# A new hand-written order of steps for a fused attention and ReGLU kernel, and a separate buffer for its last output columns

## The chip, the cores and the metric

The kernel runs on one core of a Trainium2 chip. The metric is the device time of one execution in microseconds (us). A core has five engines that run side by side, each working through its own queue of instructions in order: TensorE (PE in the profile; its weight loads are PEld), VectorE (DVE), ScalarE (ACT), GpSimd (POOL) and SyncE (SP, which here only issues transfers). Transfers issued by SP and ACT show in the profile as hardware queues (q1, q10), those issued by POOL as the software queue (q0).

## The reference

```
def phi(x):
    proj = np.einsum('bhsd,df->bhsf', x, w_phi)            # d = 64, f = 128
    proj = proj - np.max(np.abs(proj), axis=-1, keepdims=True)
    return np.concatenate([np.exp(proj), np.exp(-proj)], axis=-1)
q_p, k_p = (phi(q), phi(k))                                # q, k, v: [8, 8, 576, 64]
kv = np.einsum('bhsf,bhsd->bhfd', k_p, v)
z = np.sum(k_p, axis=2)
num = np.einsum('bhsf,bhfd->bhsd', q_p, kv)
den = np.einsum('bhsf,bhf->bhs', q_p, z)[..., None] + 1e-06
x = (num / den).transpose(0, 2, 1, 3).reshape(4608, 512)
out = (np.maximum(x @ w_gate, 0) * (x @ w_val)) @ w_out    # 512 -> 1536 -> 512
```

Eight batches of linear attention with an exponential feature map feed a gated feed-forward layer over 4608 tokens. Inputs and output are float32; the products run in bfloat16.

## The kernel before, in words

The work is cut into 1427 small steps. The code registers them under keys, such as `("fv", 1, 0)`, and a string `ORDER` of step numbers (a planner searched it by annealing under a cost model of its own) says in which order they are written into the program. Each step puts its instructions at the end of the queues of the engines that it uses, so `ORDER` fixes the order inside each engine, and the engines wait for each other through semaphores. A mark `'` behind a number takes the step's other engine, where it has two. A word `z4` puts four dummy matmuls on zeros there.

Steps by key, with their lines in the profile:

- `ld`: a load. `v` and `vm` (value rows) are issued by SP; `k`, `q`, `km`, `qm` and the weights (`wv0` to `wv2`, `wg0` to `wg2`, `wo`) by POOL, since they are cast to bfloat16 on the way (L214, L220, L236, L243, L252). Batch 0's k and v are loaded ahead of the order, by SP, k in float32 into the buffer that v of batch 1 takes afterwards. `v2` takes the buffer of `v0`.
- `turn`: a transpose of q or k by DMA, issued by SP (batches 2 to 7, L292, and the tails, L298). Batches 0 and 1 are turned on PE (`kT`, `qT`, L271) and copied out of PSUM (`kTc`, `qTc`, L284, on DVE or ACT).
- `kr`, `qr` (L312), `qc` (L543): the feature products on PE; `km`, `qm` (L319): row maxima on DVE; `ke`, `qe` (L368, L561): the exponentials on ACT; `kk`, `qk` (L379, L577): the exponentials `ek`, `cq` of the maxima on ACT.
- `vs`, `vsm` (L328, L410, L395): value rows times `ek`, the "scalings", on POOL or DVE. Both operands lie in SBUF.
- `kv` (L482, L505): PE sums keys times values; `kvc` (L418) copies the sums out on ACT or DVE.
- `n` (L591): PE products of queries with those sums; `nt`, `nu` (L610, L622) combine them on DVE; `xu` (L629, L631): a reciprocal on DVE and the division on POOL or DVE; `xd` (L639): a DMA transpose of the result into `xT`, issued by SP (batches 0 and 1 use PE, `xT` and `xc`, L271 and L651).
- `fv`, `fg` (L721, with the copy L736 on ACT or DVE, and L743 on DVE): the value and the gate half of the first feed-forward product, for group g of 512 tokens and one of 12 slices of 128 columns. Group 0 runs its first eight pairs on 256 tokens each; its pairs 0 to 7 read `wv0` and `wg0`, 8 to 11 `wv1` and `wg1`, 12 to 15 `wv2` and `wg2`.
- `fo` (L769, copy L779, store L750 or L754): the second product, in three thirds of four matmuls for each 128 tokens. Groups 0 to 7 are the batches' first 512 tokens; group 8 takes the last 64 of every batch, and its last 128 tokens are done in two parts, columns 0 to 351 and 352 to 511.

The attention of batch b + 1 is laid between the feed-forward products of group b, so PE's queue alternates between both. `out_sb`, which holds output rows until they are stored, has two buffers in turn.

Of the kernel before, what the change touches and what calls it, by code (L numbers as in the profile page):

```python
# [8 lines left out]
FP32 = mybir.dt.float32  # L9
# [13 lines left out]

ORDER = """7 z4 82 92 8 83' 93' 84 87 86 88 94 97 95 99 100 98 96 0 85 89 102 103 101' z1 104 108 105 90' z1
112 122 106 107 109 29 110 113' 114 111' 115 123' 124 118 126 132 127 117 119 91 128 133 125 120 z3
148 149 187 188 134 137 135 116 129 156 151 160 155 158 153 121 10 130 142 143' 131 190 192 136 139
144' 194 150 152 157 161 138 140 154 196 159 198 189 191 200 141 145 147' 162 1 146 54 193 175 176
163 266 267' 164 177 2 195 165 166 169 170 167 171 168 181 182 199 3 226 172 178 214 201 179 183 9  # L30
# [5 lines left out]
284 288 1118' 1119 286 1120 1121 274 292 323 325 285 287 289 265 264 279 280 361 363 281 327 276  # L36
291 360 365 278 277' 293 30 295 329 333 1122 297 303 296 304 298 305 331 39 312 1123 1124 300 301
335 348 351 299 302 352 353 51 313 349 364 366 314 1125 306 1126 315 316 317 342 354 355 350 356 12
357 362 1127 1128 343 344 309 310 311 318 1129 367 368 373 358 359' 374 375 369 339 340 40 1130
# [9 lines left out]
522 515 491 521 493 520 494 1171 1172' 492 1173 1174' 1175 19 1176 516 519 570 574 572 495' 528 532  # L49
# [3 lines left out]
543 549 1189 1190 1191 636 638 550 599 598 603 551 602 1192' 1193 1194 601 582 583 561 562 637 579  # L53
580 600 1195 1196 640 605 604 639 641 606 607 584 1197 1198 1199 626 630 581 72 585 586 616 617 646
650 1200 620 36 1201 629 618 45 643 647 649 651 652 1202 1203 648 608 1204 1205 35 627 631 619 621
609 691 610 623 695 663 667 628 22 46 657 622' 661 659 1206 1207 632 611 665 653 612 693 613 614
1208 1209 1210' 662 666 615 656 660 692 1211 1212' 696 694 658 56 664 1213 1214 1215 624 625' 633
634 635 736 737 697 701 698 700 642 1216' 1217 740 73 644 645' 699 680 739 654 655 1218 702 675 668
681 682 721 703 722 723 738 1219 1220 672 676 1221 669 673 677 707 683 684 21 674 708 670 671 678
679 685 718 719 720 1222 1223 1224 1225 1226 25 741 742 686 687 688 709 743 1227 715 716 717 689'  # L60
690 1228 766 768 756 53 757 23 770 746 747 749 748 1229 1230 760 1231 1232 710 750 704 705 706 711
1233 759 1234 712 713 1235 751 752' 773 775 714 724' 725 761 763 726 802 804 1236 1237' 728 730
1238 1239 777 727 729 1240 1241 731 806 732' 758 767 772 776 771 762 801 769 1242 1243' 753 744
745' 805 754 774 803 764 765 755 733 734 735' 37 837 808 810 807 812 841 809 1244' 1245 1246 813 48
47 820 821 1247 778 811 1248 26 839 814 815 816 785 786 822 817 818 787 779 780 781 819 1249 796
1250 1251 1252 797 836 840 838 74 798 77 823 824 75 1253 790 791 1254' 1255 793 24 794 795 76 831
# [5 lines left out]
935 939 881 964 1287 906 81 966 967 968 28 50 965 937 1288' 1289 934 1290 1291 1292 936 974 977 976  # L72
870 938 940 941 975 994 1293 997 862 863 852 996 872 873 978 995 882 883' 1294' 1295 1296 979 981
907 908 999 910 942 943 1297 853 1000 944 998 913 914 909 915 969 1298 1299 945 1300 911 912 916
921 922 924 925 1301 948 1001 980' 1302 1303 1304 949 57 917 926 946 918 1002 1003 923 950 947 959
919 1305 960 956 920 927 928 961 957 958 1306 971 982 983 951' 952 953 984 986 988 954 955 1004
# [43 lines left out]
def kernel(  # L120
# [32 lines left out]
    E = D + 1  # L153
# [11 lines left out]
    sb_f = ctx.enter_context(tc.tile_pool(name="sb_f", bufs=3))  # L165
# [5 lines left out]
    sb_g = ctx.enter_context(tc.tile_pool(name="sb_g", bufs=4))  # L171
# [540 lines left out]
    def ffn(g):  # L712
# [45 lines left out]
        for t in range(4):  # L758
            cols = LAST if g == B and t == 3 else ((0, DM),)
            for part, (c0, c1) in enumerate(cols):  # L760
                for third in range(3):

                    @atoms.add("fo", g, t, part, third)
                    def _(alt, t=t, part=part, third=third, c0=c0, c1=c1):
# [14 lines left out]
                        copy_by(copy_of(alt, "ACT", "DVE"))(out_sb, po)  # L779
                        store(t, out_sb, c0, c1)  # L780

# [25 lines left out]

    atoms.run(ORDER, keep_busy)
# [28 lines left out]
```

## Time and profile before

| | us |
|---|---|
| median of 3 runs (385.54 to 386.85) | 385.89 |
| the profiled execution's own time | 386.66 |
| its span, first to last instruction | 384.9 |
| PE busy | 365.2 (95%) |
| DVE busy | 298.4 (78%) |
| ACT busy | 223.3 (58%) |
| POOL busy | 140.8 (37%) |

Busy time is the time in which an engine had an instruction in work; PE's includes 9 dummy matmuls, and the ends of matmuls are modelled.

### The profile page before, as it was taken

To read this page: it belongs to the slowest core of one execution; us is meant where nothing else is said; L and a number is where in the kernel's file an instruction comes from. 1 tells how busy PE (TensorE), PEld (TensorE's weight loads), DVE (VectorE), ACT (ScalarE), POOL (GpSimd) and SP (SyncE) were. 2 spreads that over 40 slices of the span, in tenths; PEclk is the share of its full clock that TensorE was granted. 3 is DMA by queue.
4 is the path that set the end of the run, shared out by engine and by line. 5 is a ranking of instruction groups with operands and counts; after the bars stand their busy time and mean duration, and the time that the engine had idled before them with its cause. 6 is when DMAs were issued, how large, how long until landed. Compare 5 with 4: busy or idle time off the path is not lost.

```text
span 384.9 us, 8951 instructions
## 1 busy us (share of the span) xinstructions
PE 365.2 (95%) x3457; PEld 196.2 (51%) x3505; DVE 298.4 (78%) x639; ACT 223.3 (58%) x524; POOL 140.8 (37%) x178
## 2 busy tenths in 40 slices
PE   6779999999998999899999999999999999999995
PEld 2567455545544645465555544455554544444443
DVE  7998897988888899888998897998958734834520
ACT  7898794769476847874875539774663403201111
POOL 5775742447462327742550227815501110000000
PEclk9899999999999999999999999999999999999999
DMA  8999993995199994974947825863310130021003
GB/s 256 186 240 207 206 153 78 211 175 103 52 187 164 186 153 72 165 136 114 147 119 160 178 29 151 164 98 42 96 56 3 28 111 27 2 66 57 2 17 93
DMA packets 87930, 45.11 MB, mean 117 GB/s; under 512 B 55824, under 2 KB 82000, under 8 KB 87888
## 3 DMA queue, kind: packets, MB, share of 16 engines
q1 hardware_dynamic: 60208, 30.42, 35.8%
q0 software_dynamic: 27200, 13.57, 28.1%
q8 instruction: 27, 0.44, 0.5%
q10 hardware_dynamic: 480, 0.56, 0.5%
q14 instruction: 15, 0.12, 0.1%
HBM read 37.78 MB, written 9.44 MB: 123 GB/s over the span
## 4 chain that ended last, share of the span: by engine, by line
PE 83%; DVE 6%; DMA 5%; ACT 3%; issue 2%; POOL 1%; SPq 0%; DVEq 0%
PE pa L721 47%; PE pa L769 21%; PE pa L591 5%; PE pa L482 4%; PE pa L312 3%; DMA wg_sb<-in_moe_w_gate_dram 3%; DMA xT<-xu 2%; PE pa L543 2%; ACT kp L368 2%; DVE vs L328 2%; DVE mk L319 1%; DVE t L610 1%; DVE u L622 1%; DMA out_dram<-out_sb 1%; DVE mq L319 1%
## 5 line engine op out<-in xcount | busy, mean ns | idle before, releaser
L721 PE MATMUL pa<-xT,wv_sb 128*128 128x512 bf16 (+1 forms) x384 | 98.3, 370 | 2.6 <-DMA xT<-xu 1.4
L721 PE MATMUL pa<-xT,wg_sb 128*128 128x512 bf16 (+1 forms) x385 | 97.7, 370 | 2.1 <-DVE h L743 0.8
L769 PE MATMUL pa<-wo_sb,h 128*128 128x512 bf16 (+2 forms) x429 | 97.4, 373 | 1.2 <-issue 0.5
L743 DVE SCALAR_TENSOR_TENSOR h<-pa,val_sb 128x512 bf16<-128x512 f32 (+1 forms) x112 | 74.2, 668 | 31.4 <-PE pa L721 26.1
L736 ACT CAST val_sb<-pa 128x512 bf16<-128x512 f32 (+1 forms) x75 | 43.0, 573 | 82.1 <-PE pa L721 81.1
L561 ACT ACTIVATE qp<-pa 128x512 bf16<-128x512 f32 x144 | 76.7, 626 | 9.9 <-PE pa L543 7.7
L368 ACT ACTIVATE kp<-pa 128x512 bf16<-128x512 f32 (+1 forms) x152 | 77.4, 593 | 8.1 <-PE pa L312 7.3
L631 POOL TENSOR_TENSOR xu<-u,r 128x512 bf16<-128x512 f32 x30 | 31.1, 1040 | 135.3 <-DVE r L629 72.2
L328 POOL TENSOR_TENSOR vs<-vn,ek 128x512 bf16<-128x512 f32 (+1 forms) x58 | 59.4, 1036 | 33.7 <-ACT ek L379 30.5
L721 PEld LDWEIGHTS <-wv_sb 128*128 128x128 bf16 x448 | 41.8, 98 | 46.5 <-DVE mk L319 1.9
L721 PEld LDWEIGHTS <-wg_sb 128*128 128x128 bf16 x448 | 41.6, 98 | 45.8 <-issue 2.1
L769 PEld LDWEIGHTS <-h 128*128 128x128 bf16 x444 | 41.2, 98 | 46.0 <-issue 1.1
L319 DVE TENSOR_REDUCE mk<-pa 128x4 f32<-128x512 f32 (+1 forms) x76 | 46.8, 650 | 3.9 <-PE pa L312 3.3
L319 DVE TENSOR_REDUCE mq<-pa 128x4 f32<-128x512 f32 x72 | 46.2, 677 | 2.7 <-PE pa L312 2.6
L610 DVE TENSOR_TENSOR t<-pa,cq 128x195 f32<-128x195 f32 (+3 forms) x120 | 38.0, 327 | 5.4 <-ACT cq L577 3.3
L622 DVE TENSOR_TENSOR u<-pa,t 128x195 f32<-128x195 f32 (+3 forms) x120 | 37.8, 332 | 2.9
L591 PEld LDWEIGHTS <-qp 128*128 128x128 bf16 x640 | 27.6, 98 | 14.3 <-issue 2.7
L779 ACT COPY out_sb<-pa 128x512 f32<-128x512 f32 x21 | 12.6, 599 | 38.1 <-PE pa L769 36.6
L591 PE MATMUL pa<-kv,qp 128*128 128x65 bf16 x640 | 30.4, 193 | 2.2 <-issue 1.4
L736 DVE CAST val_sb<-pa 128x512 bf16<-128x512 f32 (+1 forms) x37 | 25.0, 677 | 6.1 <-PE pa L721 5.5
L779 DVE COPY out_sb<-pa 128x512 f32<-128x512 f32 (+2 forms) x16 | 10.5, 653 | 24.1 <-PE pa L769 22.8
L482 PEld LDWEIGHTS <-kp 128*128 128x128 bf16 x480 | 16.1, 98 | 2.7 <-DVE kv L418 0.4
(68 smaller groups left out, 284.4 us busy)
## 6 DMA issues: line engine op xcount, KB each, us to landing
out_dram<-out_sb SPq DMA_DIRECT2D x32, 256.0 KB, 2.5
vn<-in_v_dram SPq DMA_DIRECT2D x6, 1024.0 KB, 6.5
qn<-in_q_dram POOLq DMA_DIRECT2D x8, 512.0 KB, 8.2
kn<-in_k_dram POOLq DMA_DIRECT2D x6, 512.0 KB, 7.8
wv_sb<-in_moe_w_val_dram POOLq DMA_DIRECT2D x3, 512.0 KB, 10.9
wg_sb<-in_moe_w_gate_dram POOLq DMA_DIRECT2D x3, 512.0 KB, 9.7
wo_sb<-in_moe_w_out_dram POOLq DMA_DIRECT2D x1, 1536.0 KB, 15.3
vn<-in_v_dram SPq DMA_DIRECT2D x1, 1152.0 KB, 7.9
```

Source lines behind the costliest of these rows:

```text
L319: nc.vector.tensor_reduce(m, some.rearrange("p (c f) -> p c f", f=F), axis=AX.X, op=ALU.max, apply_absolute_value=True,)
L328: eng.tensor_tensor(dst[:, :, s, 0:D], src, ek[:, :, s : s + 1].to_broadcast(list(src.shape)), op=ALU.mult,)
L368: nc.scalar.activation(st["kp"][:, s, 0 : n // 2, par, :], st["banks"][par][:, 0 : n // 2 * F].rearrange("p (a f) -> p a f", f=F), AF.Exp, ...
L482: nc.tensor.matmul(kv_ps[:, hh, s, :], lhsT=lhsT, rhs=rhs, start=(n == 0), stop=(n == 19))
L561: nc.scalar.activation(x["qp"][:, s, slot].rearrange("p a b -> p (a b)"), st["cols", i][par], AF.Exp, scale=sign,)
L591: nc.tensor.matmul(pn[:, E * (2 * i + s) : E * (2 * i + s + 1)], lhsT=x["qp"][:, s, slot, blk, :], rhs=kv_of(b, lo + i)[:, s, :],)
L610: nc.vector.tensor_tensor(x["t", j][rows, 0:n], ab[:, :, 1], c[:, :, None].to_broadcast([np_, n, E]), op=ALU.mult,)
L622: nc.vector.tensor_tensor(x["u"][rows, lo : lo + n], ab[:, :, 0], x["t", j][rows, 0:n], op=ALU.add)
L721: nc.tensor.matmul(ps, lhsT=w[:, dc, P * fi : P * fi + P], rhs=xTs[g][:, dc, lo:hi], start=(dc == 0), stop=(dc == NDC - 1),)
L736: copy_by(copy_of(alt, "ACT", "DVE"))(st["val", n], ps)
L743: nc.vector.scalar_tensor_tensor(st["h2"][:, fi, lo:hi], ps, 0.0, st["val", n], op0=ALU.max, op1=ALU.mult)
L769: nc.tensor.matmul(po, lhsT=st["h2"][:, fi, P * t : P * t + P], rhs=wo_sb[:, fi, c0:c1], start=(fi == 0), stop=(fi == NFC - 1),)
```

## The change

`ORDER` is replaced as a whole. The set of steps is the same, and so is the broad plan: counted along PE's queue, the first `fv` of every group stands within two matmul groups of where it stood. What differs is the order inside that plan, and the engine of some steps:

| steps | before | after |
|---|---|---|
| `kTc` on ACT / DVE | 8 / 3 | 5 / 6 |
| `kvc` on ACT / DVE | 19 / 13 | 12 / 20 |
| `fv` copies on ACT / DVE | 75 / 37 | 71 / 41 |
| `fo` copies on ACT / DVE | 21 / 16 | 22 / 15 |
| `xc` on ACT / DVE | 5 / 3 | 4 / 4 |
| `xu` division on POOL / DVE | 30 / 6 | 28 / 8 |
| `vs` on POOL / DVE | 58 / 12 | 59 / 11 |
| dummy matmuls | 4, 1, 1, 3 | 3, 1, 6 |

The planner that made the new order no longer lets a scaling on VectorE run while GpSimd works, and it serves transfers in order of their arrival.

The loads of the opening and of the second group in their order (P: POOL's queue, S: SP's queue; `xd 2 1` is a quarter of batch 2's result, the store is of group 1):

```
before  P: q0 k1 (vs 0 1 0) wv0 qm0 (vs 0 2 0) (vs 0 0 1) (vs 0 3 0, 0 3 1) q1 (vs 0 4 0 .. 0 5 1) wg0 wv1 wg1 (xu, xu) wv2 (xu, xu) wg2 wo k2
        S: turn-qm0 v1 turn-k2 ...        later: xd 2 1, v3, xd 2 0, turn-qm1, xd 2 3, store, xd 2 2
after   P: q0 k1 wv0 qm0 (vs 0 0 1) (vs 0 2 1, 0 2 0) (vs 0 3 0, 0 3 1) q1 (vs 0 4 0 .. 0 5 1) wg0 wv1 (xu, xu) wg1 km1 (xu, xu) wv2 wg2 wo k2
        S: turn-qm0 v1 vm1 v2 turn-km1 turn-k2 ...  later: v3, v4, xd 2 0, xd 2 2, store, xd 2 1, xd 2 3
```

The other edit gives the last 160 output columns a buffer of the pool of `u`, which is idle by then:

```
-                        out_sb = sb_g.tile([P, DM], FP32, name="out_sb", bufs=2)[:, 0 : c1 - c0]
+                        if part:
+                            out_sb = sb_f.tile([P, H, E], FP32, name="u").rearrange("p h e -> p (h e)")
+                        else:
+                            out_sb = sb_g.tile([P, DM], FP32, name="out_sb", bufs=2)
+                        out_sb = out_sb[:, 0 : c1 - c0]
                         copy_by(copy_of(alt, "ACT", "DVE"))(out_sb, po)
                         store(t, out_sb, c0, c1)
```

The start of the string, before and after:

```
-ORDER = """7 z4 82 92 8 83' 93' 84 87 86 88 94 97 95 99 100 98 96 0 85 89 102 103 101' z1 104 108 105 90' z1
+ORDER = """z3 82 83' 92 93' 94 97 7 8 98 95 99 84 87 86 96 0 102 103 88 85 z1 104 105 107 100' 122 112 89 90'
...
```

More of the change, by code (lines that the diff above doesn't have):

```diff
@@ L54 @@
[L54 to L65, printed above, removed]
@@ new lines @@
+163 164 177 195 199 31 166 167 169 170 168 165 178 256 226 227' 171 179 1 257' 2 172 181 182 180
+246 266 217 236 12 183 220 267 184 201 282 221 197 218 222 219 214 215 173 283' 205 237 216 321
+174' 185 186 322' 202 203 3 30 208 209 223 210 206 204 207 211 238 240 1092 1093 1094 239 4 247 242
+1095 1096 224 225' 1097 1098' 5 212 213 6 11 324 326 241 328 228 232 1099 1100 230 1101 1102' 229
+1103 1104 1105 1106 231 233 1107 1108 243 244 245 268 269 248 271 13 258 234 270 259 250 1109 262
+1110' 251 249 253 261 273 274' 263 272 1111 1112 252 1113 1114' 1115 264' 260 255 1116 1117 284 330
@@ new lines @@
+332 290 288 334 235 292 1118 294 1119 1120' 1121 286 254 323 327 285 289 287 276 361 363 278 277
+325 365 51 265 275 279 280 329 331 281' 291 39 295 360 40 293 296 1122 300 303 301 302 304 297 333
+298 305 299 306 1123 1124 335 354 355 356 312 313 351 1125 362 309 310 339 340 336 364 337 341 314
+307 308' 315 366 316 317 311 1126 1127 338 342 352 353 318 343 344 345 367 368 369 348 373 374 349
+1128 375 1129 319 320' 1130 1131 350 1132 357 378 398 401 379 382 14 381 408 410 400 41 16 42 358
+359 1133 1134 409 346 347 402 1135 399 411 413 414 370 371 380 372 1136' 412 1137 1138' 1139 58 60
@@ new lines @@
+59 403 388 425 427 429 1140 389 62 391 1141 1142 1143 393 383 404 61 33 52 1144 1145 1146' 392 419
[5 rows of a table added]
+1167 514 55 499 19 510 537 529 533 503 502 44 534 536 488 491 1168' 1169 1170 531 490 515 564 568
+492 518 520 538 521 489 493 505 519 1171' 522 523 504 506 507 494 1172 1173 1174 528 532 530 570
+574 516 517' 572 566 575 1175 1176 1177 569 573 571 66 525 69 67 71 563 567 1178' 1179 524 526 43
+527' 540 1180' 544 495 496 565 35 376 547 548 549 497' 558 559 560 1181 590 68 545 546 70 1182 1183
+591 1184 555 556 593 557 552 22 541 542 20 553 554 587 588 592 561 562 594 595 589 1185 1186 1187
@@ new lines @@
+1188 543 1189 550' 598 602 599 551 601 600 636 603 604 1190' 1191 639 1192 579 1193 638 1194' 1195
+637 640 1196 580 576 577 578 46 596 641 605 606 607 582 583 584 34 1197 597 643 1198 1199 626 581
+585 586 646 649 648 627 629 647 628 616 630 1200 1201' 1202 651 652 608 45 620 617 619 377 1203
+1204 1205 609 621 610 1206 663 618 667 691 56 657 695 622 661 650 1207' 665 1208 1209 653 611 612
+1210' 642 623 631 633 659 693 613 614 615 1211 1212 1213 1214' 662 664 656 692 694 36 666 1215 696
+1216' 1217 658 668 660 1218' 698 700 697 699 736 740 72 624 625' 737 654 655 702 739 23 644 632 634
@@ new lines @@
+635' 701 645' 1219 1220' 703 707 708 672 715 718 716 741 709 717 1221 53 721 719 722 720 1222 723
+738 680 681 675 724 676 1223 686 687 688 21 677 710 25 1224 682 1225 1226 711 673 674 725 712 669
+670 671 743 1227 1228 766 768 73 756 759 746 749 1229 47 1230' 678 679 760 770 1231 758 748 683 684
+685 704 705 706 1232 747 751 752 757 1233 1234 1235 689 726 801 803 690 805 802 727 761 729 728
+713' 714 1236 1237' 806 750 804 730 753' 1238 1239 731 733 1240' 767 769 771 773 754 732 755 1241
+1242 1243 775 777 734 808 37 810 772 776 774 807 811 763 1244' 48 1245 1246 742 812 813 735 762 764
@@ new lines @@
+765' 809 1247 744 74 745 78 836 837 75 839 76 1248' 841 1249 1250 828 77 79 81 820 829 830 1251 817
+814 815 816 1252 1253 840 825 1254 818 821 838 831 832 27 822 826 827 819 38 57 782 1255 1256 1257
+1258 778 833 790 779 780 783 784 834' 842 849 850 851 1259 1260 1261 1262 781 1263 846 28 847 793
[4 rows of a table added]
+1285 50 1286' 1287 1288 880' 964 967 965 935 939 930 932 934 937 966 892 893 968 862 1289 1290' 863
[3 rows of a table added]
+955 970 921 922 923 927' 928 1304 1305 951 952 1306 1004 1008 984 987 985 1006 1046 956 989 957 991
@@ new lines @@
+1048 1050 958 962 963 986 1307 1308 1002 1003 979 1309' 1310 1010 1014 1005 1009 980 981 1012 988
+1040 1044 1042 1007 1311 1312 1051 982 983' 972 973' 1011 1015 1045 1039 1047 990 1049 1041 1313
+1043 992 993' 1013 1016 1314 1315 1316 1317 1318' 1319 1020 1069 1070 1320' 1017 1018 1019 1071
+1063 1064 1065 1023 1321 1024 1025 1066 1067 1322 1021 1022 1026' 1027 1323 1324 1325 1068 1034
+1035 1036 1055 1326 1327 1328' 1074 1078 1076 1075 1329 1056 1052 1053 1330' 1057 1331 1332 1031
+1032 1058 1059 1060 1333 1334 1054 1061 1062 1335 1336' 1337 1338' 1339 1028 1072 1073 1029 1030
@@ L91 @@
+1033 1037 1038 1340 1341 1342' 1343 1344 1345 1346 1347 1348 1087 1349 1077 1079 1080 1350 1351
[4 rows of a table added]
+1418 1419 1420 1421 1422 1423 1424 1425 1426'"""
 class Atoms:
```

27 lines of the change are left out of this document (3 added, 24 removed), and 42 rows, old and new, of the table ORDER.

## The prediction

> **What bounds the kernel now.** I read the busy times first, then the busy time of each engine by stretches of 10 us, then every idle gap of PE after the opening.
>
> ```profile
> PE 365.2 (95%) x3457; PEld 196.2 (51%) x3505; DVE 298.4 (78%) x639; ACT 223.3 (58%) x524; POOL 140.8 (37%) x178
> ...
> 10.00:20.00 10.00, 7.82 (x149) 5.16 (x150) 10.00 (x18) 8.75 (x25) 7.86 (x11) 0.83 1.32 183
> 20.00:30.00 10.00, 8.04 (x193) 6.57 (x193) 9.20 (x32) 10.00 (x24) 6.01 (x9) 1.00 1.22 244
> ...
> 110.00:120.00 10.00, 8.44 (x67) 3.89 (x66) 8.38 (x15) 8.22 (x23) 5.24 (x7) 1.00 1.01 171
> ...
> 350.00:360.00 10.00, 9.95 (x48) 4.52 (x47) 6.39 (x10) 1.17 (x2) 0.00 (x0) 1.00 0.07 28
> ```
>
> The last four rows give, after the length, the busy time of PE, PEld, DVE, ACT and POOL, PE's granted clock, the DMA share and GB/s. From 10 to 30 us PE is busy 15.9 of 20 us while DVE and ACT reach 10.00 of 10: there the attention's vector work sets the pace. Later PE is full (9.95 in 350 to 360), and only a gap in PE's work, or less of it, moves the end. The new order has the same matmuls but one dummy more. So its whole possible gain lies in the opening, in the gaps, and behind the last matmul. The gaps above 0.3 us (in brackets, with what ended them):
>
> ```profile
> 30.68 0.61 PE L721 MATMUL pa<-xT,wg_sb 128*128 128x256 bf16 x4 [0.36 <-DMA wg_sb<-in_moe_w_gate_dram]
> 58.58 0.64 PE L591 MATMUL pa<-kv,qp 128*128 128x65 bf16 x15 [1.37 <-issue]
> 118.01 1.02 PE L721 MATMUL pa<-xT,wv_sb 128*128 128x512 bf16 x4 [1.41 <-DMA xT<-xu]
> 160.16 1.02 PE L721 MATMUL pa<-xT,wg_sb 128*128 128x512 bf16 x4 [0.37 <-DVE mq L319]
> 163.49 1.02 PE L721 MATMUL pa<-xT,wg_sb 128*128 128x512 bf16 x4 [0.56 <-DVE h L743]
> ```
>
> They add to 4.1 us. That is about all that a better order can win between 30 and 380 us.
>
> **The change, term 1: the opening.** Group 0's first gate half needs `wg0` (the 0.36 us gap). Its load waits in POOL's queue behind batch 0's scalings.
>
> ```profile
> 9.86 2.34 DVE L328 TENSOR_TENSOR vs<-vn,ek 128x512 bf16<-128x512 f32 x1 [0.41 <-ACT ek L379]
> 14.39 2.06 POOL L328 TENSOR_TENSOR vs<-vn,ek 128x512 bf16<-128x512 f32 x2 [2.12 <-ACT ek L379]
> 20.90 0.82 POOL L243 DMA_DIRECT2D wg_sb<-in_moe_w_gate_dram  x1
> 20.88 0.40 SPq L220 DMA_DIRECT2D vn<-in_v_dram  x1
> 29.71 0.60 PE L721 MATMUL pa<-xT,wv_sb 128*128 128x256 bf16 x4 [0.18 <-ACT tT L284]
> DMA to landing us min/median/max: 8.5/9.7/13.2
> ```
>
> The one long scaling on DVE (2.34 us, while POOL scaled too) holds up the maxima behind which POOL then idles 2.12 us. In the new order POOL takes this scaling and DVE a half-size one. On POOL that trades a step of about half of 2.06 / 2 = 1.03 us for a whole one, some 0.5 us more, against 2.12 us of waiting of which part remains: `wg0` is issued about 0.7 us sooner (0 to 1.5). ACT, full from 20 to 30 us, loses three `kTc` copies to DVE.
>
> ```profile
> L284 ACT CAST tT<-pa 128x512 bf16<-128x512 f32 x2 | 1.1, 595 | 0.0
> L284 ACT COPY tT<-pa 128x512 bf16<-128x512 bf16 x2 | 1.3, 832 | 0.0
> L284 ACT COPY tT<-pa 128x256 bf16<-128x256 bf16 x1 | 0.6, 552 | 0.0
> ```
>
> That is 0.60 + 0.83 + 0.55 = 2.0 us, DVE's own list there growing less than the 2.34 us that it lost. So `fv 0 0` could start 0 to 1.8 us before 29.71. It gains only if `wg0` is there. Its landing hangs on who is served first, which the queues by themselves show (transfers from 22 to 23 and from 24 to 25 us; packets, MB, share):
>
> ```profile
> q1 hardware_dynamic: 406, 0.11, 124.5%
> q0 software_dynamic: 45, 0.02, 15.7%
> ...
> q1 hardware_dynamic: 161, 0.37, 101.6%
> q0 software_dynamic: 1, 0.00, 0.6%
> ```
>
> Here `v1` (q1), issued at the same moment as `wg0` (q0), went first and alone; `wg0` landed 9.7 us after its issue. In the new order `v1` again waits in SP's queue behind `turn-qm0`, which waits for a load of unchanged place, so its issue stays at 20.9. With `wg0` 0.7 us sooner the two are a tie (its issue takes 0.82 us). If `v1` still goes first, `wg0` lands at 30.6 as before and nothing is gained; if not, up to 1.8 us. The second burst of dummies, six for three, may hold the turning of q back: nine dummies took
>
> ```profile
> L200 PE MATMUL pa<-zeros 128*128 128x512 bf16 x9 | 4.1, 575 | 1.0 <-DVE zeros L798 1.0
> ```
>
> 4.1 us, so three more are up to 1.4 us of PE, partly beneath its waits there. I take -0.5 us (bounds -1.8 and 0), nearest to the tie that is lost. The Trainium skill, "DMA: Bandwidth & Descriptors", section "Queues, rings and completion order", says that each DMA engine goes round robin between the queues it has work for, packet by packet; by that rule q0 should have kept moving beside q1, and 0.00 MB in a whole microsecond disagrees. By the rule the opening would gain the whole 1.8 us.
>
> **Term 2: batch 2's result.** The 1.41 us gap:
>
> ```profile
> 102.83 0.57 SPq L214 DMA_DIRECT2D vn<-in_v_dram  x1
> 110.30 7.47 DMA xT<-xu
> ```
>
> `v3` was issued among the four `xd` of batch 2, two more transposes and a load of k came beside them, and the last `xd` took 7.47 us. In the new order `v3`, `v4` and `k4` are issued ahead of the first `xd`, and both tail transposes leave the group. In SP's queue the four `xd` have only stores between them. Counted along PE's queue the last `xd` keeps 9.7 us to its reader (9.6 before), so it need only land in less than that. I take -1.4 us, the gap's whole length (bounds -1.4 and 0). What is late next there is nothing that I can name.
>
> **Term 3: the end.**
>
> ```profile
> 369.92 10.55 PE L769 MATMUL pa<-wo_sb,h 128*128 128x512 bf16 x60
> 378.50 2.64 DMA out_dram<-out_sb
> 381.32 0.32 DVE L779 COPY out_sb<-pa 128x160 f32<-128x160 f32 x1 [1.06 <-DMA out_dram<-out_sb]
> ```
>
> PE ends at 369.92 + 10.55 = 380.47, yet the last copy waits until 381.32, for the store of the rows two copies back. With a buffer of its own it starts at about 380.5: -0.8 us (bounds -0.85, and -0.3 if ACT, which now copies the 352 columns and issues both parts' second halves, comes last).
>
> **Term 4: what the order costs elsewhere.** DVE gets dearer.
>
> ```profile
> L736 DVE CAST val_sb<-pa 128x512 bf16<-128x512 f32 x36 | 24.6, 684 | 6.1 <-PE pa L721 5.5
> L418 DVE CAST kv<-pa 128x260 bf16<-128x260 f32 x13 | 5.4, 419 | 1.5 <-PE pa L482 1.5
> L631 DVE TENSOR_TENSOR xu<-u,r 128x512 bf16<-128x512 f32 x6 | 5.2, 866 | 0.2
> L328 DVE TENSOR_TENSOR vs<-vn,ek 128x512 bf16<-128x512 f32 x10 | 13.5, 1347 | 2.6 <-ACT ek L379 2.6
> 230.00:240.00 10.00, 9.95 (x59) 4.44 (x59) 7.46 (x12) 9.75 (x27) 6.97 (x9) 1.00 0.58 145
> 240.00:250.00 10.00, 9.66 (x111) 5.30 (x110) 9.43 (x19) 7.13 (x16) 8.93 (x13) 1.00 0.77 155
> 250.00:260.00 10.00, 9.89 (x123) 5.81 (x124) 9.46 (x18) 7.36 (x18) 1.04 (x1) 1.00 0.61 97
> ```
>
> Four `fv` copies, seven `kvc`, two `xu` and three `kTc` come, one `vs` and one `fo` copy go: 4 x 0.68 + 7 x 0.42 + 2 x 0.87 + 3 x 0.5 - 1.35 - 0.7, about +7 us in 385 us. Most lies under PE's matmuls, as DVE's 298 us do. The densest place is the change from group 4 to group 5 (230 to 260 us): there the new order puts four scalings of batch 6 on DVE that were POOL's, and one division more, 4 x 0.87 (one as long as the division, nothing beside it) to 4 x 1.35, plus 0.87, that is 4.4 to 6.3 us onto 26.4 of 30 us. 30.8 to 32.7 us of work do not fit into 30: 0.8 to 2.7 us over, of which the slack before 230 may take some. I take +0.8. The small DVE gaps (0.37, 0.56) belong to the old order; the new one will have its own, and I count them as unchanged. The 1.37 us gap has no releaser, and I leave it.
>
> Sum: -0.5 - 1.4 - 0.8 + 0.8 = -1.9 us. Against the profiled execution's 386.66 us that gives 384.8; the median of the runs is 385.89, so 384.0.
>
> **Rivals.** *The value loads get ahead* (slower). Behind `v1` the new SP queue holds `vm1` and `v2`, which came only behind the first stores before. If hardware-queue transfers are served ahead of POOL's whatever their arrival, `wg0` waits for all of them:
>
> ```profile
> vm<-in_v_dram SPq DMA_DIRECT2D x6, 128.0 KB, 4.7
> vn<-in_v_dram SPq DMA_DIRECT2D x6, 1024.0 KB, 6.5
> ...
> 19.34 1.30 SPq L298 DMA_TRANSPOSE qmT<-qm  x1
> ...
> q0 software_dynamic: 326, 0.16, 121.9%
> ```
>
> 2 x 128 + 1024 KB, 1.31 MB, at the 0.37 MB in 1 us quoted for `v1` are 3.5 us on the first gate half, or on `wg1`, which is now issued behind two divisions. It decides if `wg0` has not begun when `v2` is issued, at about 22 us. For it: q0 stood still for `v1`. Against it: q0's earlier load still moved 0.16 MB from 21 to 22 us (the last row), though SP's transpose had been issued at 19.3. The time is 385.9 - 1.4 - 0.8 + 0.8 + 3.5 = 388.0; if it costs only 2.5 us, 387.0.
>
> *DVE becomes the bound at the change to group 5* (no change): the whole 2.7 us over, and no gain in the opening: 385.9 - 1.4 - 0.8 + 2.7 = 386.4; with half of that, 385.0.
>
> *The queues share, or `wg0` wins the tie* (faster): then `wg0` is in before PE reaches it, and the opening gains 1.8: 385.9 - 1.8 - 1.4 - 0.8 + 0.8 = 382.7; without the DVE cost 381.9. The sharing is the rule of the page named above.
>
> *The order does not do what it says*: a late transfer stalls another `xd`, as 1.4 us did here, and only the end remains: 385.1.
>
> **How the numbers follow.** A measurement of this kernel tells about 0.3% (1.2 us) from no change: faster is below 384.7, slower above 387.0. Chances: the forecast 0.38 (383.0 to 385.0), the sharing or the won tie 0.12, DVE as bound 0.15, only the end 0.09, the value loads ahead 0.26 (mostly above 387.0, a part of it milder). Faster: 0.33 of the forecast, 0.12 and 0.03 of the others, 0.48. Slower: 0.24 of the value loads, 0.04 of DVE, 0.28. The same: 0.24. Cases of both signs count, so the range goes from 381.9 to 388.0.
>
> **What would show it.** Right: in the profile after, `fv 0 0` at 28 to 30 us and `wg0` landing no later than 30.7; no gap of PE before the first matmul of group 2 (near 118 us); the last DVE copy within 0.2 us of PE's last matmul. Wrong: a gap of PE above 1 us ended by `wg_sb` in 30 to 42 us (the value loads), a DVE row of 10.00 with PE below 9.5 in 230 to 260 us (DVE), or any gap ended by `xT<-xu`.

## The result, and the profile after

The changed kernel takes 391.35 us (median of 6 runs, 389.77 to 393.37) against 386.44 us for the kernel before beside it: 1.2 % slower, ratio 1.0123 with a 95 % interval of 1.0085 to 1.0162. A second measurement gave 1.0109 (1.0086 to 1.0133). The forecast was 384.0 us. The profiled execution took 391.72 us (span 389.9) against 386.66 (384.9).

The busy times of the page after, and three of its stretches of 10 us (busy PE, PEld, DVE, ACT, POOL, then PE's granted clock, DMA share, GB/s):

```profile
PE 373.1 (96%) x3506; PEld 198.7 (51%) x3506; DVE 301.8 (77%) x651; ACT 218.1 (56%) x510; POOL 138.6 (36%) x180
...
10.00:20.00 10.00, 8.89 (x137) 5.70 (x136) 7.92 (x15) 7.60 (x21) 6.77 (x9) 1.00 1.23 171
...
60.00:70.00 10.00, 8.28 (x91) 4.68 (x91) 6.00 (x21) 4.80 (x11) 1.04 (x1) 0.83 0.84 115
...
240.00:250.00 10.00, 7.32 (x56) 3.11 (x54) 9.29 (x16) 6.46 (x16) 5.56 (x7) 1.00 0.52 146
```

PE is full in most stretches, as before. The new losses stand at 60 to 70 us, where PE idles and then runs at a clock of 0.83, and at 240 to 250 us, where it is busy 7.32 of 10 us. The rows of PE, DVE and POOL that carry them, in order of time (the bracket is the idle time before, and what ended it):

```profile
9.07 2.33 DVE L328 TENSOR_TENSOR vs<-vn,ek 128x256 bf16<-128x256 f32 x3
...
12.13 0.61 PE L312 MATMUL pa<-w,tT 64*128 64x128 bf16 x8 [1.11 <-DVE tT L284]
...
13.15 2.76 PE L200 MATMUL pa<-zeros 128*128 128x512 bf16 x6
...
15.71 1.91 PE L271 MATMUL pa<-ident,qn 128*128 128x128 bf16 x16
...
22.31 0.82 POOL L243 DMA_DIRECT2D wg_sb<-in_moe_w_gate_dram  x1
...
31.95 0.60 PE L721 MATMUL pa<-xT,wv_sb 128*128 128x256 bf16 x4 [0.24 <-ACT tT L284]
...
61.72 0.62 PE L591 MATMUL pa<-kv,qp 128*128 128x65 bf16 x15 [2.03 <-issue]
...
240.52 0.69 DVE L328 TENSOR_TENSOR vs<-vn,ek 128x512 bf16<-128x512 f32 x1 [2.38 <-DMA vn<-in_v_dram]
...
242.80 0.54 PE L591 MATMUL pa<-kv,qp 128*128 128x65 bf16 x12 [1.62 <-DVE out_sb L783]
...
246.08 1.04 PE L721 MATMUL pa<-xT,wg_sb 128*128 128x512 bf16 x4 [1.02 <-DVE mk L319]
...
386.23 0.32 DVE L783 COPY u<-pa 128x160 f32<-128x160 f32 x1 [7.18 <-PE pa L769]
```

The first val product starts at 31.95 us; the row shown before had 29.71. Two gaps of the old order are gone: no gap above 0.3 us stands at 110 to 125 us (1.41 before) or at 160 to 170 us (0.37 and 0.56 before).

To see where the time went, each weight load of PE was put beside the same step of the other kernel, since both do the same steps in another order. The table gives, at some points of PE's own work, how much later than that work PE is, in us; the difference of two rows is what PE lost between them. The work is counted at one price for each size of matmul, so a single row can be off by some tenths.

| up to | before | changed | lost more by the change |
|---|---|---|---|
| first val product of group 0 | 11.3 | 13.4 | +2.1 |
| `fg 0 14` (about 52 us) | 11.3 | 13.5 | +0.1 |
| `n 1 1 1 1` (about 63 us) | 13.2 | 17.8 | +2.3 |
| `kv 2 1` (about 96 us) | 13.5 | 18.7 | +0.6 |
| `fv 2 2` (about 124 us) | 14.4 | 17.9 | -1.7 |
| `fo 4 2 0 2` (about 236 us) | 14.9 | 17.3 | -1.1 |
| `fv 5 3` (about 249 us) | 15.5 | 21.0 | +3.1 |
| `fv 8 11` (about 370 us) | 15.8 | 21.2 | -0.1 |

Behind the last matmul 0.6 us are won. Three places lose 7.5 us, two win 2.8.

### The profile page after: what moved, and what is told of

It is laid out like the page before. It is cut to its first block, busy times and chain, and to the rows that moved or that the text cites. A ratio compares the mean times of both kernels' runs of the same rounds, so it can differ in the third digit from the quotient of the medians.

```text
span 389.9 us, 8975 instructions
## 1 busy us (share of the span) xinstructions
PE 373.1 (96%) x3506; PEld 198.7 (51%) x3506; DVE 301.8 (77%) x651; ACT 218.1 (56%) x510; POOL 138.6 (36%) x180
## 4 chain that ended last, share of the span: by engine, by line
PE 78%; DVE 7%; DMA 6%; issue 4%; POOL 2%; ACT 1%; SPq 0%; POOLq 0%; DVEq 0%
PE pa L721 42%; PE pa L769 20%; PE pa L482 4%; PE pa L312 4%; PE pa L591 4%; DMA wg_sb<-in_moe_w_gate_dram 3%; DMA vn<-in_v_dram 2%; PE pa L543 2%; DVE vs L328 2%; PE pa L271 1%; DVE mk L319 1%; DVE h L743 1%; ACT kp L368 1%; DVE u L622 1%; DVE t L610 1%
## 5 line engine op out<-in xcount | busy, mean ns | idle before, releaser
L721 PE MATMUL pa<-xT,wg_sb 128*128 128x512 bf16 (+1 forms) x400 | 100.0, 373 | 1.6 <-DVE mk L319 1.0
L743 DVE SCALAR_TENSOR_TENSOR h<-pa,val_sb 128x512 bf16<-128x512 f32 (+1 forms) x112 | 73.8, 667 | 35.5 <-PE pa L721 32.7
L769 PE MATMUL pa<-wo_sb,h 128*128 128x512 bf16 (+2 forms) x444 | 99.9, 376 | 0.0
L721 PE MATMUL pa<-xT,wv_sb 128*128 128x512 bf16 (+1 forms) x400 | 99.3, 371 | 0.3 <-ACT tT L284 0.2
L736 ACT CAST val_sb<-pa 128x512 bf16<-128x512 f32 (+1 forms) x71 | 40.8, 574 | 79.9 <-PE pa L721 75.5
L368 ACT ACTIVATE kp<-pa 128x512 bf16<-128x512 f32 (+1 forms) x152 | 76.6, 595 | 8.3 <-PE pa L312 5.3
L328 POOL TENSOR_TENSOR vs<-vn,ek 128x512 bf16<-128x512 f32 (+1 forms) x59 | 60.3, 1032 | 55.3 <-ACT ek L379 45.7
L631 POOL TENSOR_TENSOR xu<-u,r 128x512 bf16<-128x512 f32 x28 | 29.1, 1042 | 106.9 <-DVE r L629 69.9
L783 ACT COPY out_sb<-pa 128x512 f32<-128x512 f32 (+1 forms) x22 | 13.0, 589 | 49.9 <-PE pa L769 45.3
L591 PEld LDWEIGHTS <-qp 128*128 128x128 bf16 x640 | 27.8, 98 | 16.9 <-issue 5.7
L736 DVE CAST val_sb<-pa 128x512 bf16<-128x512 f32 (+1 forms) x41 | 27.7, 675 | 4.3 <-PE pa L721 2.8
L379 ACT ACTIVATE ek<-mk 128x8 f32<-128x8 f32 (+1 forms) x76 | 11.8, 220 | 10.1 <-DVE mk L319 10.0
```

Of the source, the lines that this page charges most:

```text
L328: eng.tensor_tensor(dst[:, :, s, 0:D], src, ek[:, :, s : s + 1].to_broadcast(list(src.shape)), op=ALU.mult,)
L368: nc.scalar.activation(st["kp"][:, s, 0 : n // 2, par, :], st["banks"][par][:, 0 : n // 2 * F].rearrange("p (a f) -> p a f", f=F), AF.Exp, ...
L591: nc.tensor.matmul(pn[:, E * (2 * i + s) : E * (2 * i + s + 1)], lhsT=x["qp"][:, s, slot, blk, :], rhs=kv_of(b, lo + i)[:, s, :],)
L721: nc.tensor.matmul(ps, lhsT=w[:, dc, P * fi : P * fi + P], rhs=xTs[g][:, dc, lo:hi], start=(dc == 0), stop=(dc == NDC - 1),)
L736: copy_by(copy_of(alt, "ACT", "DVE"))(st["val", n], ps)
L743: nc.vector.scalar_tensor_tensor(st["h2"][:, fi, lo:hi], ps, 0.0, st["val", n], op0=ALU.max, op1=ALU.mult)
```

## The experiments

Words in an order are the numbers of its steps; a mark behind a number stands for the second engine. "Ratio" is to the kernel before, run beside it. The files of most experiments count one line less than the kernels at the same step (L327 is L328).

**One repair each.** All four are the changed kernel with one edit.

```diff
e1_kr3_copy_back   -124 108 113 114   +124 108 113' 114
e2_three_dummies   -111 z6 148        +111 z3 148
e3_v6_early        -1265 24 788       +832 24 27
e4_values_late     -199 31 166  -236 12 183   +1125 12 362  +42 31 358
```

> The changed kernel with one mark put back: the copy kTc 0 3 goes to ScalarE again, as in the kernel before. Theory (the copy's seat on VectorE, behind three half scalings, set the late opening): kr 0 3 starts at once instead of 1.11 us late, q's transposes, q1's load and wg0 follow some 1.1 us sooner, the first val product starts near 30.5 us (31.65 with the whole change, 29.34 before), and the time is near 390.3. Rival (six dummies are the cause): the burst still covers it, first val product within 0.3 us of 31.65, time 391.3. Rival (v1's load ahead of wg0 sets the opening): PE's chain is sooner, but wg0 lands no sooner, and the first gate product stays near 32.7.

> The changed kernel with three dummy matmuls ahead of q's transposes instead of six, as in the kernel before. Theory (the six hold the turning of q back): q's transposes start 0.65 us (3 x 0.215) to 1.4 us sooner than 15.71, wg0's issue moves with them from 22.31, the first val product comes at 30.3 to 31.0, time 390 to 390.7. Rival (the late key chain alone is the cause, the dummies lie beneath it): first val product within 0.3 us of 31.65, time 391.3.

> The changed kernel with the load of v6 moved ahead of v7's on SyncE's queue, so that it no longer stands behind the two transposes xd 5 3 and xd 5 2. Theory (v6 lands late at 240.4, its first scaling waits 2.38 us at the head of VectorE's queue and PE loses 1.62 and 1.02 us behind it): both PE gaps go, PE's loss between 240 and 246 us falls by 2.6 to 2.8, time 388.6. Rival (VectorE's density at the change from group 4 to 5 is the bound): the gaps go to other VectorE work in 240 to 260, time within 0.6 of 391.3.

> The changed kernel with the loads of vm1 and v2 back behind the first stores, where the kernel before had them. Theory: the DMA engines are then done with wo, k2 and q2 some 5 us sooner, PE's fetch of instructions (one 16 KB packet on each engine of the group's queue for 256 of them) is no longer kept waiting at 59 us, the gap of 2.03 us without a releaser at 61.7 falls to 1.4 or less, PE does not run at half clock for 3.4 us after it, and wg0 lands sooner as well: loss up to 66 us smaller by 2.4 to 3.5, time 388 to 389. Rival (the gap is a matter of the place in the program, every 256 instructions, whatever the DMA does): gap still 2.0 within 0.2 at the same n 1 0 0 matmuls, time within 0.6 of 391.3.

Beside them the changed kernel once more, as it is:

> The changed kernel as it is, once more, as a yardstick for the kernels with one edit each, beside the same runs of the kernel before. Expected: 1.2 % slower than the kernel before, within the interval of the first measurement (0.9 to 1.6 %). If it came out near 0.7 %, the single repairs so far (0.6 to 0.8 % slower) would have gained nothing that the time shows, and only their traces would speak for them. Theory on instruction fetch: a gap without a releaser of 1.6 to 2.1 us at n 1 0 0 again, since the order of loads is the same; half clock after it may or may not come.

The ratios are to be compared, not the medians: the kernel before took 387.14 us beside e1 to e4 and 386.42 beside c1.

| kernel | median us | ratio (95 %) |
|---|---|---|
| c1_change_again | 391.32 | 1.0109 (1.0086 to 1.0133) |
| e1_kr3_copy_back | 391.14 | 1.0081 (1.0049 to 1.0113) |
| e2_three_dummies | 389.69 | 1.0066 (1.0040 to 1.0091) |
| e3_v6_early | 390.46 | 1.0076 (1.0048 to 1.0104) |
| e4_values_late | 389.51 | 1.0064 (1.0036 to 1.0091) |

Each repair lies below the yardstick, by 0.3 to 0.45 %; only those of e2 and e4 come near to standing clear of it. The traces tell more. Four timelines: PE's dummies and q's transposes in e2; PE in the opening of e1; PE in e4 at `n 1 0 0` and after it; DVE and PE in e3.

```profile
13.80 1.49 PE L199 MATMUL pa<-zeros 128*128 128x512 bf16 x3
15.08 1.91 PE L270 MATMUL pa<-ident,qn 128*128 128x128 bf16 x16
```

```profile
11.84 0.61 PE L311 MATMUL pa<-w,tT 64*128 64x128 bf16 x8 [0.85 <-ACT tT L283]
...
31.53 0.50 PE L270 MATMUL pa<-ident,qn 128*128 128x128 bf16 x6 [1.73 <-issue]
```

```profile
60.54 0.82 PE L590 MATMUL pa<-kv,qp 128*128 128x65 bf16 x16
...
93.74 0.19 PE L481 MATMUL pa<-vsm,kp 128*128 128x65 bf16 x1 [0.91 <-POOL vsm L394]
```

```profile
239.49 1.26 DVE L327 TENSOR_TENSOR vs<-vn,ek 128x512 bf16<-128x512 f32 x1 [1.02 <-ACT ek L378]
...
244.62 1.04 PE L720 MATMUL pa<-xT,wg_sb 128*128 128x512 bf16 x4 [0.88 <-DVE mk L318]
```

The dummies: three take 1.49 us and six 2.76 us, and nothing hides the difference of 1.27 us; the first val product of e2 starts at 31.38 us (31.95 in the changed kernel, 32.72 in c1). The copy: on ScalarE it stands behind two exponentials (1.11 us), so PE resumes 0.3 us sooner and not 1.1; that expectation fell: giving the copy back to ScalarE is not enough where the exponentials stand ahead of it. The load of v6: the wait for it is gone and PE's loss there falls by 1.8 us; a gap of 0.88 us remains, behind VectorE's scalings of 1.0 to 1.3 us beside GpSimd. The value loads: the gap without a releaser is gone (no bracket at 60.54) and no half clock follows, but vm1, now behind the turning of q3, comes late for `vsm` (0.91). `wg0` took 10.6 us to land, no less than with the value loads in front of it (9.8 to 12.1 in five profiles); that part of the expectation fell.

**Where the gap without a releaser comes from.** The trace has a DMA queue of its own for instructions, with 27 packets of 16 KB in the span: one for about 260 of PE's 7,010 matmuls and weight loads. Its row stands in the microsecond in which the packet for this place was served, first of the kernel before (55 to 56 us), then of the changed one (59 to 60 us):

```profile
q0 software_dynamic: 496, 0.06, 97.3%
q1 hardware_dynamic: 652, 0.16, 75.1%
q8 instruction: 1, 0.02, 7.1%
```

```profile
q0 software_dynamic: 369, 0.19, 138.4%
q8 instruction: 1, 0.02, 6.1%
```

The packet came while the other queues filled the DMA engines. It ended at 57.12 us before and PE resumed at 58.58; it ended at 60.25 after and PE resumed at 61.72. Sixteen gaps of 1.3 to 2.4 us between two weight loads, in 13 of the 16 profiles, end 1.2 to 1.6 us after the end of such a packet. Thirteen stand at the same place of PE's program: before its 733rd weight load in the old order, its 735th in the new. The three others (e1, e3, e6) stand some 765 instructions earlier, three packets' worth, at 28 to 32 us, while a value load runs. Kernels with less in the queues at that time tell whether the loads are the cause:

```diff
e7_q2_late (kernel before)       -261 13 252   +12 13 357
```

> The kernel before with the load of q2 moved on GpSimd's queue from behind k2's to behind xu 1 0 0, about 30 us later, where nothing needs it before 80 us. Theory (PE's fetch of instructions waits behind queued bulk loads): wo, k2 and km1 are through by about 53.5 us instead of 56, the fetch starts 2 us sooner, before PE has run out of instructions, and the gap of 1.37 us at n 1 0 0 of the kernel before goes: 1.4 to 1.8 us faster in all after it. Rival (a gap at that place of the program whatever the DMA engines do): gap 1.3 to 1.5 us still there.

```profile
58.68 0.64 PE L590 MATMUL pa<-kv,qp 128*128 128x65 bf16 x15 [0.87 <-issue]
```

0.87 us against 1.37, ratio 0.9984 (0.9965 to 1.0004): a third of what was expected. The large loads were gone (18 GB/s at 50 to 52 us), but k2's turning and km1's load then filled the engines at 54 to 56 us (share 1.49), just when the packet was due. Neither side was shown; f1, at the end of this section, has less queued at that time.

**All four repairs.**

```diff
e5_four_repairs   -124 108 113 114   +124 113' 108 114
                  and e2_three_dummies, e3_v6_early, e4_values_late
```

> The changed kernel with four repairs together: three dummies instead of six ahead of q's transposes; kTc 0 3 on ScalarE and directly behind kTc 0 4 there, ahead of the exponentials ke 0 2 1; vm1's and v2's loads behind the first stores; v6's load ahead of v7's. Theory (each loss has its own cause and they add): opening sooner by 1.3 (dummies) and 0.8 (kr 0 3 at about 11.0 instead of 12.1), no gap without a releaser near 60 us and no half clock (2.6), the wait on v6 gone (1.9, with some 0.9 of VectorE's scalings left at 245): together 6.6, so 384.8 us, 0.4 % faster than the kernel before. Rival (the losses are in series with a common bound, and what is won early is lost later): less than half of it, 388 to 390.

386.36 us, ratio 0.9994 (0.9973 to 1.0015): all of the yardstick's loss of 1.09 % (4.2 us) is back, about two thirds of the expected 6.6 us. The instruction packet started at 55.7 and no gap above 0.3 us stands at `n 1 0 0`. With three dummies, and the copy ahead of ScalarE's exponentials, q's transposes start at 14.06 us (15.08 in e2, 15.71 in the changed kernel), and the first val product starts at 30.47 (29.71 in the kernel before). What was not expected is vm1:

```profile
14.06 1.91 PE L270 MATMUL pa<-ident,qn 128*128 128x128 bf16 x16
...
92.94 0.19 PE L481 MATMUL pa<-vsm,kp 128*128 128x65 bf16 x1 [2.15 <-POOL vsm L394]
```

**Two parts of the change alone, on the kernel before.**

```diff
e6_buffer_only        the new buffer for the last output columns, order as before
e8_before_buffer_v3   the same, and  -452 15 437   +451 15 42
```

> The kernel before with the one edit of the end alone: the copies of the last output columns go to a buffer u of their own pool instead of the pair of out_sb buffers. The forecast's third term says the last copy no longer waits for a store and the end comes 0.8 us sooner: 0.4 to 0.8 us faster, last VectorE copy within 0.2 us of PE's last matmul. Rival (the stores drain one after another on the DMA queue, so the end does not move): no change within 0.2 us.

> The kernel before with two of the change's gains alone: the last output columns in a buffer of their own, and v3's load moved ahead of the turning of q3 on SyncE's queue, so that it no longer collides with the transposes xd 2 1 and xd 2 0. The forecast's second term: the gap of 1.41 us before the first matmul of group 2 goes; its third term: 0.8 at the end. Both true: 384.2 to 384.8 us, 0.5 % faster than the kernel before, no PE gap over 0.3 at 113 to 118 us. Rival (the transposes are late for another reason, VectorE's xu say): gap still 1.2 or more.

PE's and DVE's rows of e6 at the end, and of e8:

```profile
381.27 3.65 PE L768 MATMUL pa<-wo_sb,h 128*128 128x512 bf16 x28
...
385.02 0.33 DVE L782 COPY u<-pa 128x160 f32<-128x160 f32 x1 [0.32 <-PE pa L768]
```

```profile
58.61 0.64 PE L590 MATMUL pa<-kv,qp 128*128 128x65 bf16 x15 [1.96 <-issue]
...
115.93 0.40 PE L311 MATMUL pa<-w,kT 64*128 64x128 bf16 x7 [0.39 <-DVE mq L318]
...
117.71 1.02 PE L720 MATMUL pa<-xT,wv_sb 128*128 128x512 bf16 x4 [0.41 <-DVE mq L318]
```

The profiled execution of e6 took 390.38 us against its median of 386.20: it has an instruction gap at 29.8 us and a stretch at half clock, of which more below. In e6 the copy starts 0.1 us after PE's last matmul (384.92), and the end of the span comes 3.69 us after that matmul instead of 4.42: 0.73 us. The time agrees (ratio 0.9984), but its interval (0.9962 to 1.0006) reaches over no change. In e8 no `xd` is waited for, but two gaps of 0.4 us behind VectorE stand there, the instruction gap is 1.96 us instead of 1.37, and the time does not fall: 1.0023 (0.9990 to 1.0056). The expected 0.5 % did not come. The gap of 1.41 us itself is not fixed: e7, with the same steps at that place, has 0.81, e6 has 1.13 ended by VectorE, and e11 below none.

```diff
e11_scalings_on_vector (kernel before)   -871 +871'   -860 +860'   -890 +890'
```

> The kernel before with one part of the change alone: the scalings vs 6 1 1, vs 6 0 0 and vs 6 3 0 on VectorE instead of GpSimd. The forecast's fourth term (VectorE too dense at the change from group 4 to 5): PE loses 0.8 more between 236 and 246 us, 387.2 us; bounds 0 to 2.7. Rival (the loss there in the changed kernel was the late v6 alone): no more than 0.2.

```profile
242.22 0.71 DVE L327 TENSOR_TENSOR vs<-vn,ek 128x512 bf16<-128x512 f32 x1
...
242.99 0.30 PE L481 MATMUL pa<-vs,kp 128*128 128x65 bf16 x4 [3.36 <-DVE vs L327]
```

1.0 % slower (1.0058 to 1.0150), 4 us, above the bound of 2.7. This is not density: VectorE takes this scaling only behind four pairs of result steps that stand ahead of it in its queue (239.10 to 242.2). In the old order it has the wrong seat, so this run says nothing on what the seats of the new order cost; e3's 0.88 us does.

**Six repairs.** To e5, vm1's load behind v2's and the three scalings back on GpSimd:

```diff
e9_six_repairs   -42 31 358 +12 31 362   -871' +871   -860' +860   -890' +890
```

> The changed kernel with the four repairs of e5_four_repairs and two more: vm1's load directly behind v2's (in e5_four_repairs it stood behind the turning of q3 and PE waited 2.15 us for the scaling vsm at 92.9), and the scalings vs 6 1 1, vs 6 0 0 and vs 6 3 0 back on GpSimd. Theory: PE's gap of 2.15 goes, loss at 238 to 246 us falls by a further 0.9: 386.4 - 3.0 = 383.3, 0.8 % faster than the kernel before. Rival for the scalings (GpSimd at 1.05 us each becomes the late one): a PE gap of 0.5 to 2 at 240 to 246 ended by POOL vs, time 384 to 386.

382.80 us, ratio 0.9892 (0.9864 to 0.9920): 1.1 % faster than the kernel before, and with it the version that beats both. The 2.15 us are gone, and no gap above 0.3 us is left at 238 to 250 us, so GpSimd is not late. The instruction gap is back, since PE came to it 1.3 us sooner than in e5:

```profile
59.08 0.53 PE L590 MATMUL pa<-kv,qp 128*128 128x65 bf16 x12 [1.42 <-issue]
```

**A load more.**

```diff
e10_extra_load        (e9)   -13 258   +13 1427 258    (1427: the extra load)
f2_extra_load_later   (e9)   -275 279  +275 1427 279
```

> e9_six_repairs with one more load of 512 KB (a third of the gate weights, to a place in memory that nothing reads) on GpSimd's queue right behind q2's. PE's, VectorE's and ScalarE's programs are the same. Theory (fetch of instructions waits behind queued loads): the queue is empty some 2.6 us later than 56, the fetch that started at 55.7 in e5_four_repairs starts at 58 to 59, and a PE gap without a releaser of 1.0 to 2.3 us is back at n 1 0 0: time 1 to 2.5 us above e9_six_repairs, or 4 if PE falls to half clock behind it. Rival (that gap comes from something else): no gap over 0.5 there, time within 0.5 of e9_six_repairs.

> e9_six_repairs with the extra load of e10_extra_load issued behind GpSimd's string of scalings (at 50 us) instead of ahead of it (at 43). Theory on the scaling (VectorE's scaling beside GpSimd ends only when GpSimd lets go): GpSimd's string is as in e9_six_repairs, the scaling at 44.2 takes 1.4 us and not 5.3, and the PE gap of 3.2 us at 50 is gone. Theory on the fetch: the extra 512 KB keep the queue full 2 to 2.6 us longer, so the fetch starts at 57.5 to 59.5 and the gap is 2 us or more: time 1 to 2.6 us above e9_six_repairs, 384 to 385.4. Rival (the load itself stops PE): the 3.2 us gap at 50 stays, time near 388.

e10 took 387.98 us, 5 us more than e9, and not for a longer instruction gap (1.14 us). DVE's and PE's rows of e10, POOL's of e10, then the same scaling of DVE in e9 and in f2:

```profile
44.15 5.28 DVE L328 TENSOR_TENSOR vs<-vn,ek 128x256 bf16<-128x256 f32 x1
...
50.08 1.02 PE L721 MATMUL pa<-xT,wg_sb 128*128 128x512 bf16 x4 [3.21 <-DVE h L743]
```

```profile
43.81 2.06 POOL L328 TENSOR_TENSOR vs<-vn,ek 128x512 bf16<-128x512 f32 x2
45.81 0.25 POOL L410 CAST vs<-ek 128x16 bf16<-128x16 f32 x1
45.96 1.04 POOL L328 TENSOR_TENSOR vs<-vn,ek 128x512 bf16<-128x512 f32 x1
46.95 0.24 POOL L410 CAST vs<-ek 128x16 bf16<-128x16 f32 x1
47.10 2.04 POOL L328 TENSOR_TENSOR vs<-vn,ek 128x512 bf16<-128x512 f32 x2
49.10 0.44 POOL L410 CAST vs<-ek 128x16 bf16<-128x16 f32 x1
```

```profile
44.23 1.41 DVE L327 TENSOR_TENSOR vs<-vn,ek 128x256 bf16<-128x256 f32 x1
```

```profile
44.50 1.41 DVE L327 TENSOR_TENSOR vs<-vn,ek 128x256 bf16<-128x256 f32 x1
...
59.68 0.53 PE L590 MATMUL pa<-kv,qp 128*128 128x65 bf16 x12 [1.75 <-issue]
```

Issuing the load (0.66 us of GpSimd) pushed GpSimd's string of scalings back by 0.6 us, and VectorE's scaling of half size beside it took 5.28 us, until the string's third small copy, instead of 1.41. PE stood for 3.21 us and then ran at half clock for 3.4 us, which makes up most of the 5 us. With the same load behind the string (f2) it takes 1.41 again and the gap of 3.21 us is gone: the load was not it. f2's time is 384.17 us, 1.4 above e9, inside what was expected; its instruction packet starts at 57.5 instead of 56.8 and the gap is 1.75 instead of 1.42, short of the 2 us expected.

**Nothing queued when the instructions are due.**

```diff
f1_q2_turned_late (e9)   -271 13 258  +306 13 1123    -360 40 293  +31 40 362
```

> e9_six_repairs with q2's load behind xu 1 0 0 on GpSimd's queue and q2's turning behind vm1's load on SyncE's queue, so that neither is queued at 54 us, when PE comes within some 210 instructions of the end of what it holds. Theory (fetch waits behind queued loads): the fetch starts 1 us or more sooner than 56.8, the gap of 1.42 at n 1 0 0 falls below 0.6, and the time is 1 to 1.5 us below e9_six_repairs (382.8), so 381.5. Rival (the gap is there whatever is queued): gap 1.2 to 1.6, time as e9_six_repairs or later, if q2 comes late.

The DMA engines moved 25 GB/s from 54 to 56 us. There is no gap at `n 1 0 0`:

```profile
58.74 0.66 PE L590 MATMUL pa<-kv,qp 128*128 128x65 bf16 x16
```

As a mark for how late a packet is, take the point 215 instructions before the place of the gap: the packet before this one started 212 to 220 instructions before PE would have run out, in all sixteen profiles. In f1 the packet started at 56.5, 1.0 us behind that mark (2.7 in e9). The profiles agree on this: where the packet starts 0.3 to 1.2 us behind the mark (e5, f1, e4) there is no gap, and where it starts 1.9 to 3.1 us behind it (the thirteen others) there is one. The theory holds there. The price stands elsewhere:

```profile
76.14 3.27 PE L768 MATMUL pa<-wo_sb,h 128*128 128x512 bf16 x8 [4.18 <-ACT out_sb L782]
```

SyncE waited for q2 (until 68.4) with the first stores behind it, so the output buffers stayed full and PE stood for 4.18 us: 390.86 us in all, ratio 1.0117 (1.0082 to 1.0152).

## Why the prediction was wrong

**Term 1, the opening: wrong in sign, and the first step that failed.** Forecast -0.5 (-1.8 to 0), measured about +2. Of the kernels with the old steps there, before, e7, e8 and e11 load the weights of the first val product at 29.3 to 30.5 us (mean 29.8); the changed kernel does so at 31.7 and 32.4 in its two profiles (mean 32.0). (e6, 31.2, and e3, 33.7, have an instruction gap of 1.4 and 1.8 us just before.) Two things were mis-sized. The dummies were priced right (1.4 at most, 1.27 measured) and then put "partly beneath its waits": none of it was. And the copies that move to VectorE were counted as a gain, with three half scalings there as cheaper than the long one that left. But one of these copies, `kTc 0 3`, is the one that PE waits for, and the scalings stand ahead of it: with the small copy behind them they held VectorE for 2.1 to 3.9 us in the six profiles of these steps (c1 and e1 to e4 among them). Putting right both, as e5 and the four kernels built on it do, brings the first weights back to 29.7 to 30.1 us. `wg0` was then issued at 22.3 us, later and not sooner, and landed at 32.65 where 30.7 was the mark set. A gain by the freed ScalarE did not show.

**Term 2, batch 2's result: right.** The gap is gone in every kernel with the new order. As a price 1.4 was on the high side: in the old order it varies from 0 to 1.41.

**Term 3, the end: right.** -0.8 forecast, 0.6 and 0.7 measured behind the last matmul. The copy follows PE by 0.1 us.

**Term 4, VectorE at the change from group 4 to 5: place right, size right in part by luck, a wait missed.** +0.8 forecast, 0.88 left in e3, gone in e9 with the scalings back on GpSimd. But the forecast had 30.8 to 32.7 us of VectorE's work in the 30 us from 230 on, and in e3 it was busy 27.8 of them: it was not full over the stretch, it only came to group 5's maxima late, behind scalings of 1.0 to 1.3 us. And 3.1 us were lost, since v6's load had been put on SyncE's queue behind the transposes xd 5 3 and xd 5 2 (behind the second alone before). SyncE's rows of that load, first of the kernel before, then of the changed one:

```profile
215.93 0.58 SPq L214 DMA_DIRECT2D vn<-in_v_dram  x1
...
230.89 1.16 SPq L214 DMA_DIRECT2D vn<-in_v_dram  x1
```

It was issued 15 us later and landed 9.5 us after that, its scaling stood at the head of VectorE's queue, and the output copy behind it kept PE waiting. The working counted the movement of v3, v4 and k4 past the transposes of batch 2, and did not count the same for v6. The sign that was named, a VectorE row of 10.00, did not show (9.29): VectorE had first stood 2.38 us waiting for v6.

**The gap left alone.** "The 1.37 us gap has no releaser, and I leave it": it is an instruction fetch held up by queued loads and transposes, so moving loads was moving it. In the changed kernel it is 1.9 to 2.0 us, 0.5 us more than in the profile before; but the old order has 1.36 to 1.96 us in four profiles (mean 1.6), the new one 1.57 to 2.03 in five (mean 1.9), so the change's own part is nearer to 0.2 and not clear. The profile shown has 1.7 us on top from the half clock behind it, which is not the change's, since e6 with the old order has it too. The small VectorE gaps "counted as unchanged" were a gain of 1.1 us.

**The rivals.** The one that ended slower was right in sign and not in place. That the value loads made `wg0` slower is not shown (9.8 to 12.1 us to land with them in front, 10.6 in e4 without, 9.7 in the kernel before), and PE waited only 0.4 us for it in the changed kernel; their main effect was on the instructions. The division of the queues: from 24 to 25 us q0 moved 9 packets beside 128 of q1, so `v1`, issued first, again went ahead and the tie was not won. But from 29 to 31 us q0 moved 306 packets and q1 305: there they share, packet for packet. The row with 0.00 MB, by which the working set sharing aside, does not show that q0 had anything ready to move.

**What adds up.** Opening 2.2 and instruction gap 0.2 (by the means), v6 and VectorE 3.1, and 0.6 in the row of `kv 2 1` (a scaling of batch 2 on VectorE took 2.34 us there beside GpSimd; that this is the cause was not tried), less 1.7, 1.1 and 0.6: 2.7 us, or 4.4 in an execution with the half clock, against 4.9 between the medians. How many executions have it is not known, so 0.5 to 2.2 us stay without a place. Repairing what these steps name gives back all of the loss and, with two more, 1.1 % over the kernel before.

## What to carry to other kernels

A load that is moved in a queue takes its place behind every wait of what now stands ahead of it: list for each moved load who waits at the head of that queue, and who stands behind its reader. When a step goes to VectorE while GpSimd works on the same memory, price it by what GpSimd has in work, up to the whole string, and not by its own length. A gap of PE that nothing in the program ends is worth a look at the DMA queue of instructions before it is set aside.

## What the runs showed of the hardware

PE's instructions come through the same DMA engines as data, in the 27 packets of q8. One packet earlier, with 215 instructions left, PE takes 11 us or more for those and does not stop; here most are small matmuls with their weight loads (72 matmuls in 1.3 us), PE is through in 3 us, and a packet that starts 1.9 to 3.1 us behind the mark stops it for 0.9 to 2.0 us.

VectorE's scaling, which reads two operands from SBUF, takes 0.69 us at 512 columns and 0.41 at 256 alone. Beside GpSimd it took 1.25 and 2.34 us (512), 1.41 and, in e10, 5.28 us (256). The Trainium skill, "SBUF — State Buffer", section "Who interferes with whom", says that such an instruction and a GpSimd instruction that reads SBUF exclude each other and the second one blocks until the first is done. The trace agrees, and goes further: in e10 it stayed blocked while GpSimd went on from one instruction to the next at 45.81, 45.96, 46.95 and 47.10 us.

After gaps of PE of 1.89 us (e6), 2.03 us (changed kernel) and 3.21 us (e10), and from within one of 4.18 us (f1), PE ran at half clock for 3.4 us (the rows are the changed kernel's; after the length, PE's busy time comes first, and the clock third from the end):

```profile
62.00:63.00 1.00, 1.00 (x14) 0.50 (x11) 0.76 (x3) 0.56 (x2) 0.00 (x0) 0.64 1.21 271
63.00:64.00 1.00, 1.00 (x4) 0.37 (x3) 0.97 (x5) 1.00 (x4) 0.00 (x0) 0.50 0.67 129
64.00:65.00 1.00, 1.00 (x3) 0.29 (x2) 0.78 (x2) 0.50 (x2) 0.69 (x1) 0.50 1.16 212
65.00:66.00 1.00, 1.00 (x16) 0.66 (x15) 0.02 (x1) 0.00 (x0) 0.35 (x1) 0.65 2.59 163
```

After gaps of 1.89, 1.96, 1.98 and 3.36 us in c1, e3, e1 and e11 it did not. The Trainium skill, "TensorE: Matmul & The Clock Gate", section "What's actually happening", gives a window of about 3.4 us, idle for the fall to half clock and busy for the return: the length of the slow stretch agrees with it, the idle time needed does not, 2 us were enough. What decides between the cases is open. Seven profiles have such a stretch in the opening, between 11 and 28 us, the kernel before and c1 among them and not the changed kernel's first; what it costs there was not taken apart, so the opening of a single profile says little.
